# Two 64-row halves for small contractions, whole output rows, and later score steps in an attention-plus-mixer kernel

## The chip, the cores and the metric

The kernel runs on one core of a Trainium2 chip. The metric is the device time of one execution in microseconds (us), as the median of several runs. A core has TensorE (PE, matrix products, with its weight loads shown apart as PEld), VectorE (DVE), ScalarE (ACT), GpSimd (POOL) and SyncE (SP, which here issues most DMAs). Each engine works through its own instructions in order and waits on semaphores for the others.

## What is computed

```python
# q, k, v: (8, 8, 576, 64) float32
scores = q @ k.transpose(0, 1, 3, 2) / sqrt(64)
rel = pos[:, None] - pos[None, :]
mask_plain = (rel >= 0) & (rel < 32)                       # heads 0 to 3
mask_dil = (rel >= 0) & (rel < 128) & (rel % 4 == 0)       # heads 4 to 7
attn = softmax(where(mask, scores, -1e9))
x = (attn @ v).transpose(0, 2, 1, 3).reshape(8, 576, 512)
h = relu(x.transpose(0, 2, 1) @ w_tok1) @ w_tok2           # w_tok1 (576, 256), w_tok2 (256, 576)
u = x + h.transpose(0, 2, 1)
out = u + relu(u @ w_ch1) @ w_ch2                          # w_ch1 (512, 1536), w_ch2 (1536, 512)
```

## The kernel before

Everything is in one Python function that writes out each engine's program by hand; there is no automatic scheduler. Products are in float16 and accumulate in float32 in eight PSUM banks of 512 columns: three named `main`, three `fl` and two `sc`, each group used in turn.

**Stages of one batch.** `transposes` turns casted q and k of a pair of heads into `qz` and `kt` (contraction over 64 features of one head: the two heads of a pair sit in rows 0 to 63 and 64 to 127). Scoring makes the products of keys and queries within the few 128 x 160 blocks that a window touches (heads 0 to 3), within the four residues of 4 (heads 4 to 7, 128 x 128 blocks), and for the 64 tail rows 512 to 575. `values` (names `av`, `rec`, `xn`) multiplies by v with a column of ones, divides, and leaves x in `xn`: four blocks of 128 tokens and a fifth with the 64 tail tokens, in rows 0 to 63 of even batches and 64 to 127 of odd ones. `emit_h1` makes h (`h1p`, then a relu into `h`) in two halves of 256 columns, each for two sets `jb` of the 256 hidden tokens. `emit_u` (`up`) makes u. `gen_main` makes the gate `gt` (`gp` for 128 of the 1536 channels at a time), and the output product: `yp` in batch 0, `yx` and `yw` in `gen_out` for the others. `gen_out` uses differences of the weight blocks, `wsum_a` and `wsum_b`, which `weight_sum` computes once, on VectorE, at the end of batch 0's gating, and adds u and stores `o`.

**Scoring, twice.** From batch 2 on `scores_twin` takes q and k in other tiles (`qt`, `kr`, made by transposing DMAs) and multiplies in 64 rows of the array, the two heads of a pair in the upper and the lower half. Batches 0 and 1 use `scores_plain`, `scores_dil`, `tail_scores` and `score`: `qz` has one copy per head with the other head's 64 rows zero, so each product contracts over 128 rows; and ahead of each product a matmul of the identity with `veil` puts the mask into the bank.

**Order.** The loop over batches takes `gen_main(b)` as the main thread, and `interleave` puts between its pieces a list of steps, each with a due time on a clock of estimated costs and a cost of its own. So in the stretch of `gen_main(0)` the steps of batch 1 run (transposes, scores, values, h1, u), in that of `gen_main(1)` those of batch 2, and so on. Before the loop, batch 0's steps are written out one by one. `w4a` (named `w` in the trace, the second channel weight) comes in three DMAs of 512 KB that GpSimd issues during batch 1's casts. For batches from 2 on, u is turned by transposing DMAs on the sync queue (`utm<-u`), two column blocks of it are copied by ScalarE to `utd`, and `u_natural` turns them back (`u<-utd`) for the addition in `gen_out`.

Of the kernel before, what the change touches and what calls it, by code (L numbers as in the profile page):

```python
# [9 lines left out]
FP16 = mybir.dt.float16  # L10
# [58 lines left out]
def kernel(  # L69
# [64 lines left out]
    qza = fixed("qz", [128, 4, 2, S])  # L134
# [16 lines left out]
    w1t = [fixed(f"w1t{i}", [128, DTOK]) for i in range(2)]  # L151
# [11 lines left out]
    def emit_fixed():  # L163
        nc.gpsimd.memset(idle, 0.0)
        nc.gpsimd.memset(spread, 0.0)
        nc.vector.memset(qza[64:128, :, 0], 0.0)
# [34 lines left out]
    def load_v_steps(b):  # L201
        tn = sb.tile([128, 4, 4, D], FP32, tag="l_vn", bufs=1, name=f"l_vn_{b}")
        td = sb.tile([128, 4, 4, D], FP32, tag="l_vd", bufs=1, name=f"l_vd_{b}")
        tx = sb.tile([128, 4, D], FP32, tag="l_vx", bufs=1, name=f"l_vx_{b}")
# [12 lines left out]
        steps.append(go(tx, v[b, 4:8, 384:512, :].rearrange("h s d -> s h d")))  # L217
# [55 lines left out]
    def cast_vx(b, eng):  # L273
        copy(eng, vt[b % 2][:, :, 0:64], l32[(b, "vx")])
# [30 lines left out]
    def transposes(b, nm, hp):  # L305
# [13 lines left out]
        if b == 0:  # L319
            for h in range(2):  # L320
                rows = slice(64 * h, 64 * h + 64)
                if hp >= 2:
                    copy(eng, qz[hp][rows, h, 0:512], p[rows, 0:512])
                else:
                    copy(eng, natural(qz[hp][rows, h, 0:512]), main[rows])
# [6 lines left out]
        for h in range(2):
            rows = slice(64 * h, 64 * h + 64)
            if flat:
                copy(eng, qz[hp][rows, h], p[rows, 0:S])
            else:
                copy(eng, natural(qz[hp][rows, h]), grid[rows, :, 0:MR].rearrange("p r m -> p m r"))
# [71 lines left out]
    def first_tails():  # L409
# [7 lines left out]
        for h in range(2):  # L417
            rows = slice(64 * h, 64 * h + 64)
            nc.vector.tensor_copy(out=qza[rows, :, h, 512:S], in_=t[rows, :, 0])
        nc.vector.tensor_copy(out=kta[:, :, 512:S], in_=t[:, :, 1])  # L420

    def score(b, hp, h, out, keys, queries, hide):

        if hide is not None:
            nc.tensor.matmul(out=out, lhsT=ident, rhs=hide, start=True, stop=False)
        lhsT = keys if not isinstance(keys, slice) else kt[hp][:, keys]
        nc.tensor.matmul(out=out, lhsT=lhsT, rhs=qz[hp][:, h, queries],
                         start=hide is None, stop=True)

    def veiled(b, hp):  # L430
        return b <= 1

    def small_bank(b, hp):
        return bank("main", 3, f"sm_{b}_{hp}") if b == 0 else bank("sc", 2, f"sm_{b}_{hp}")
# [16 lines left out]
    def tail_scores(b, hp, p, c0):  # L451
        n = len(near(hp))
        for h in range(2):
            for i, x in enumerate(near(hp)):
                c = c0 + 64 * (n * h + i)
                v0 = BLK + 128 * (hp // 2) + 64 * x
                score(b, hp, h, p[:, c:c + 64], near_keys(x), slice(512, S),
                      veil[:, v0:v0 + 64] if veiled(b, hp) else None)

    def tail_exp(hp, p):  # L460
        nc.scalar.activation(
            out=tail_cols(attt[:, hp], hp),
            in_=p[:, 0:128 * len(near(hp))].rearrange("p (h x c) -> p h x c", h=2, c=64), func=AF.Exp, scale=0.125)

    def scores_plain(b, hp):
        blocks = plain_blocks(hp)
        veils = veiled(b, hp)
        for h in range(2):
            p = bank("sc", 2, f"sc_{b}_{hp}_{h}")
            for kb in range(3):  # L470
                score(b, hp, h, p[:, BLK * kb:BLK * kb + BLK], slice(128 * kb, 128 * kb + 128),
                      slice(128 * kb, 128 * kb + BLK), veil[:, 0:BLK] if veils else None)
            nc.scalar.activation(
                out=blocks[:, h, 0:3, 0:BLK], in_=p[:, 0:3 * BLK].rearrange("p (b c) -> p b c", c=BLK),
                func=AF.Exp, scale=0.125)
            yield 0.21
        p = small_bank(b, hp)
        for h in range(2):
            score(b, hp, h, p[:, 128 * h:128 * h + 128], slice(384, 512), slice(384, 512),
                  veil[:, 0:128] if veils else None)  # L480
        tail_scores(b, hp, p, 256)
        nc.scalar.activation(
            out=blocks[:, :, 3, 0:128], in_=p[:, 0:256].rearrange("p (h c) -> p h c", c=128),
            func=AF.Exp, scale=0.125)
        tail_exp(hp, p[:, 256:512])
        if not veils:
            mult(nc.gpsimd, blocks[:, :, :, 0:BLK], blocks[:, :, :, 0:BLK], band)
# [763 lines left out]
```

## Time and profile before

| | |
|---|---|
| median of 3 runs | 280.49 us (279.01 to 281.66) |
| profiled execution | 278.42 us, of which its span is 276.6 us |
| granted TensorE clock in it | 1.00 |
| TensorE busy | 265.8 us, 96% of the span, 2694 matmuls |
| VectorE, ScalarE, GpSimd busy | 168.3, 149.0, 158.8 us |
| DMA | 55.50 MB, mean 201 GB/s |

The profile is one execution. Busy times count overlapping instructions of an engine once; a matmul's shown duration includes its latency, so consecutive ones overlap, and the distance of their starts is what one costs. In the chain of work that ended last each piece is a stretch during which nothing else was waited for; a piece of n matmuls lasts n such distances.

### The profile page before, as it was taken

What the parts mean: (1) busy time and instruction counts of PE and PEld (TensorE: products, weight loads), DVE (VectorE), ACT (ScalarE), POOL (GpSimd) and SP (SyncE); (2) the same over time, 40 slices, a digit from 0 to 9 for tenths busy, and PEclk for the clock granted to TensorE, in tenths of its full rate; (3) what the DMA queues carried; (4) which work ended last, traced back from release to release, by engine and by line L of the source; (5) the groups of instructions that cost most, each with busy time, mean ns of one, the idle gap of its engine ahead of it and who ended that gap; (6) DMA issues with size and microseconds to landing.
All of it is one profiled execution on the core that took longest, in us unless ns stands there. A gap on an engine that the chain in (4) does not pass through costs nothing.

```text
span 276.6 us, 6790 instructions
## 1 busy us (share of the span) xinstructions
PE 265.8 (96%) x2694; PEld 197.2 (71%) x2694; DVE 168.3 (61%) x340; ACT 149.0 (54%) x291; POOL 158.8 (57%) x214
## 2 busy tenths in 40 slices
PE   6899999999999999997999999999999999999994
PEld 2796676897666876685775876687776866786673
DVE  6767668575568655674649454775475473961363
ACT  2864774363674465467545656476546565236500
POOL 7880760389858759849973589739980870000000
PEclk9999999999999999999999999999999999999999
DMA  7999999995979799999999999989999220553015
GB/s 216 271 248 238 291 241 210 316 241 159 343 132 226 151 316 281 233 165 259 304 221 186 257 280 255 172 156 316 304 211 148 81 79 2 99 147 78 0 40 152
DMA packets 116783, 55.50 MB, mean 201 GB/s; under 512 B 84976, under 2 KB 115696, under 8 KB 116752
## 3 DMA queue, kind: packets, MB, share of 16 engines
q1 hardware_dynamic: 112096, 49.63, 75.9%
q0 software_dynamic: 2640, 3.94, 7.9%
q10 hardware_dynamic: 2016, 1.51, 1.8%
q8 instruction: 21, 0.34, 0.5%
q14 instruction: 10, 0.08, 0.1%
HBM read 38.12 MB, written 9.44 MB: 172 GB/s over the span
## 4 chain that ended last, share of the span: by engine, by line
PE 85%; DMA 7%; DVE 4%; issue 1%; ACT 1%; ACTq 0%; POOL 0%; DVEq 0%
PE gp L934 29%; PE yx L778 12%; PE yw L778 9%; PE h1p L637 5%; PE up L649 4%; PE gt L925 4%; PE yp L961 4%; PE yp L747 3%; DMA lt<-in_k_dram 3%; PE sc L522 3%; DMA u<-utd 2%; DMA w1p<-in_moe_w_tok_dram 2%; PE h1p L635 1%; PE av L614 1%; PE av L619 1%; DVE gt L737 1%
## 5 line engine op out<-in xcount | busy, mean ns | idle before, releaser
L109 ACT ACTIVATE gt<-gp 128x512 f16<-128x512 f32 x89 | 53.2, 598 | 50.4 <-PE gp L934 50.1
L778 PEld LDWEIGHTS <-gt 128*128 128x128 f16 x600 | 57.0, 98 | 10.2 <-issue 2.0
L934 PE MATMUL gp<-utd,w 128*128 128x512 f16 x144 | 54.7, 380 | 0.0
L934 PE MATMUL gp<-utm,w 128*128 128x512 f16 x144 | 54.6, 379 | 0.0
L934 PEld LDWEIGHTS <-w 128*128 128x128 f16 x384 | 39.1, 113 | 19.8 <-issue 0.5
L115 POOL TENSOR_TENSOR attp<-attp,const 128x1280 f16<-128x1280 f16 x12 | 31.6, 2637 | 23.4 <-ACT attp L547 23.4
L737 DVE TENSOR_TENSOR gt<-gt 128x768 f16<-128x768 f16 x56 | 32.2, 605 | 12.5 <-ACT gt L109 12.2
L115 DVE TENSOR_TENSOR xn<-av,rec 128x320 f16<-128x320 f32 x64 | 31.4, 491 | 2.2
L115 POOL TENSOR_TENSOR attd<-attd,const 128x1024 f16<-128x1024 f16 x12 | 25.5, 2124 | 7.7 <-issue 5.4
L934 PE MATMUL gp<-uT,w 128*128 128x512 f16 x96 | 25.8, 380 | 0.0
L793 DVE TENSOR_TENSOR o<-yx,u 128x512 f32<-128x512 f32 x22 | 15.2, 689 | 11.2 <-PE yx L778 10.5
L778 PE MATMUL yx<-w,gt 128*128 128x256 f16 x168 | 20.6, 273 | 0.0
L778 PE MATMUL yx<-wsum_a,gt 128*128 128x256 f16 x168 | 20.6, 273 | 0.0
L547 ACT ACTIVATE attp<-sc 128x480 f16<-128x480 f32 (+1 forms) x36 | 15.9, 538 | 8.7 <-PE sc L522 8.7
L655 DVE TENSOR_TENSOR u<-up,xn 128x512 f16<-128x512 f32 x26 | 17.8, 688 | 4.1 <-PE up L649 4.1
L626 DVE RECIPROCAL rec<-av 128x5 f32<-128x5 f32 x64 | 12.2, 191 | 12.2 <-PE av L623 12.1
L105 POOL CAST c_k<-l_k 128x512 f16<-128x512 f32 x29 | 17.6, 616 | 2.2 <-DMA l_k<-in_k_dram 1.3
L863 ACT COPY utd<-utm 128x512 f16<-128x512 f16 x12 | 12.7, 1129 | 10.3 <-DMA u<-utd 6.6
L105 POOL CAST c_q<-l_q 128x512 f16<-128x512 f32 x26 | 16.3, 630 | 2.9 <-DMA l_q<-in_q_dram 2.2
L664 DVE TENSOR_TENSOR u16t<-up,xn 64x512 f16<-64x512 f32 x7 | 4.8, 689 | 21.0 <-PE up L660 21.0
L109 ACT ACTIVATE h<-h1p 128x256 f16<-128x256 f32 x31 | 11.8, 384 | 8.9 <-PE h1p L637 8.4
L798 DVE TENSOR_TENSOR o<-yw,o 128x512 f32<-128x512 f32 x13 | 9.0, 691 | 11.4 <-PE yw L778 11.3
(158 smaller groups left out, 549.6 us busy)
## 6 DMA issues: line engine op xcount, KB each, us to landing
l_q<-in_q_dram SPq DMA_DIRECT2D x15, 512.0 KB, 6.6
l_k<-in_k_dram SPq DMA_DIRECT2D x14, 512.0 KB, 7.4
out_dram<-o SPq DMA_DIRECT2D x26, 256.0 KB, 4.1
l_vn<-in_v_dram SPq DMA_DIRECT2D x32, 128.0 KB, 6.7
l_vd<-in_v_dram SPq DMA_DIRECT2D x16, 256.0 KB, 4.2
w<-in_moe_w_ch_dram POOLq DMA_DIRECT2D x6, 512.0 KB, 7.6
out_dram<-o SPq DMA_DIRECT2D x17, 128.0 KB, 2.7
l_vt<-in_v_dram SPq DMA_DIRECT2D x8, 256.0 KB, 4.7
```

Source lines behind the costliest of these rows:

```text
L105: eng.tensor_copy(out=out, in_=in_)
L109: nc.scalar.activation(out=out, in_=in_, func=AF.Relu)
L115: eng.tensor_tensor(out=out, in0=x, in1=y, op=ALU.mult)
L547: nc.scalar.activation(out=out, in_=in_, func=AF.Exp, scale=0.125)
L626: nc.vector.reciprocal(out=rec[:, :, 0], in_=av[:, :, 64])
L637: nc.tensor.matmul(out=p, lhsT=w[:, s, j], rhs=x[:, s, c], start=False, stop=(s == 3))
L655: nc.vector.tensor_tensor(out=u16(b, s), in0=blocks4(p), in1=blocks4(xn[b][:, s]), op=ALU.add)
L737: nc.vector.tensor_tensor(out=out, in0=x, in1=y, op=op)
L778: nc.tensor.matmul(out=p, lhsT=gta[:, k0 + mb, r:r + 128], rhs=weights[:, mb, c], start=(first and not mb and (not a or len(parts) > 2)), ...
L793: nc.vector.tensor_tensor(out=grid(o[(i, j)]), in0=grid(p), in1=u, op=ALU.add)
L863: nc.scalar.copy(out=natural(uTd[:, cb - 2]), in_=uTm[i][:, cb].rearrange("p r m -> p m r"))
L934: nc.tensor.matmul(out=p, lhsT=w3_block(cb, mb), rhs=uT[(b, cb)][0], start=(i == 0), stop=(i == 3))
```

## The change

1. `qz` has no zero half any more: both heads of a pair lie in one tile of 128 rows, two zeroings go, and q is copied in one instruction instead of two.
2. `scores_veiled` takes the place of the four scoring functions for batches 0 and 1. One mask matmul covers a whole bank (or each of two parts of it); the products are made in 64 rows, the two heads of a pair one behind the other into two banks, and the small blocks of two pairs share two banks. 58 matmuls per batch where there were 88. The due times of these steps are new, and the start's order is written out anew.
3. `emit_h1` makes the main four products of both `jb` first and then the 64 tail tokens for both, in 64 rows each, `jb` 0 from the upper and `jb` 1 from the lower half; both relus follow. `values` copies the tail rows to the other half, once for heads 0 to 3 and once for 4 to 7. `w1t` holds its 64 rows twice, by two DMAs, and needs no zeroing.
4. The tail of v (`l_vx`, `vt`) is loaded and cast for 64 rows only.
5. The output of a batch lies in two tiles of whole rows, single instead of four in turn. Batches 1 to 6 store each in one DMA of 512 KB where there were four of 256 KB.
6. In batch 1 one of the turned blocks of u uses another group of banks.
7. `u_natural(2)` is issued in the stretch of `gen_main(1)` instead of `gen_main(2)`.

```diff
-    qza = fixed("qz", [128, 4, 2, S])
+    qza = fixed("qz", [128, 2, 4, S])[:, 0]
...
-    w1t = [fixed(f"w1t{i}", [128, DTOK]) for i in range(2)]
+    w1t = fixed("w1t", [128, DTOK])
...
-        nc.vector.memset(qza[64:128, :, 0], 0.0)
-        nc.vector.memset(qza[0:64, :, 1], 0.0)
...
-        tx = sb.tile([128, 4, D], FP32, tag="l_vx", bufs=1, name=f"l_vx_{b}")
+        tx = sb.tile([64, 4, D], FP32, tag="l_vx", bufs=1, name=f"l_vx_{b}")
...
+    def scores_veiled(b, g):
+
+        def hide(p, c0, n, v0, w, start=True):
+            nc.tensor.matmul(out=p[:, c0:c0 + n * w].rearrange("p (x c) -> p x c", c=w), lhsT=ident,
+                             rhs=veil[:, v0:v0 + w].unsqueeze(1).broadcast_to([128, n, w]),
+                             start=start, stop=False, skip_group_check=True)
+
+        def pair(hp, banks, c0, keys, queries):
+            for h in range(2):
+                rows = slice(64 * h, 64 * h + 64)
+                q16 = qz[hp][rows, queries]
+                nc.tensor.matmul(out=banks[h][:, c0:c0 + q16.shape[-1]], lhsT=kt[hp][rows, keys], rhs=q16,
+                                 start=False, stop=True, skip_group_check=True)
+
+        n, w = (4, 128) if g else (3, BLK)
+        pairs = (2 * g, 2 * g + 1)
+        for hp in pairs:
+            ps = [bank("sc", 2, f"sc_{b}_{hp}_{h}") for h in range(2)]
+            for p in ps:
+                hide(p, 0, n, 0, w)
+            for i in range(n):
+                pair(hp, ps, w * i, slice(i, 512, 4) if g else slice(128 * i, 128 * i + 128),
+                     slice(128 * i, 128 * i + w))
...
+            yield
...
+        for p in small:
+            hide(p, 0, 2, v0, 64 * m)
+            if not g:
+                hide(p, 256, 2, 0, 128, False)
+        for j, hp in enumerate(pairs):
+            for i, x in enumerate(near(hp)):
+                pair(hp, small, 64 * (m * j + i), near_keys(x), slice(512, S))
+            if not g:
+                pair(hp, small, 256 + 128 * j, slice(384, 512), slice(384, 512))
...
         mult(nc.vector, xn[b][:, :, D * h:D * h + D], av[:, :, 0:64], rec)
-
-    def emit_h1(b, jb, half, t):
+        if h % 4 == 3:
+            c = slice(256 * (h // 4), 256 * (h // 4) + 256)
+            tail = slice(64, 128) if odd else slice(0, 64)
+            other = slice(0, 64) if odd else slice(64, 128)
+            nc.vector.tensor_copy(out=xn[b][other, 4, c], in_=xn[b][tail, 4, c])
+
+    def emit_h1(b, half, t):
...
-        p = bank("fl", 3, f"h1p_{b}_{jb}_{half}")[:, 0:256]
-        nc.tensor.matmul(out=p, lhsT=w1t[b % 2][:, j], rhs=x[:, 4, c], start=True, stop=False)
-        for s in range(4):
-            nc.tensor.matmul(out=p, lhsT=w[:, s, j], rhs=x[:, s, c], start=False, stop=(s == 3))
-        relu(nc.vector if jb and half and b == 0 else nc.scalar, t[:, c], p)
+        p = []
+        for jb in range(2):
+            p.append(bank("fl", 3, f"h1p_{b}_{jb}_{half}")[:, 0:256])
+            for s in range(4):
+                nc.tensor.matmul(out=p[jb], lhsT=w[:, s, jb:DTOK:2], rhs=x[:, s, c], start=(s == 0), stop=False)
+            if not jb:
+                yield
+        for jb in range(2):
+            rows = slice(64 * jb, 64 * jb + 64)
+            nc.tensor.matmul(out=p[jb], lhsT=w1t[rows, jb:DTOK:2], rhs=x[rows, 4, c], start=False, stop=True)
+        for jb in range(2):
+            relu(nc.vector if jb and half and b == 0 else nc.scalar, t[jb][:, c], p[jb])
+        yield
...
+        o = [fixed_o32(f"rows{i}", f"o_{b}_{i}") for i in range(2)]
...
-            store(1, 1)
             yield from product(m0 + 256, 6, wsum[4], False, w)
             with_t(1, 0, [(pw, None, None)])
-            store(1, 0)
+            store(1, every)
             yield from product(o0, 6, w4a[:, 6:12, 256:512], False, x)
             with_u(px, 0, 1)
-            store(0, 1)
+            store(0, every)
...
-            steps += score_steps(1, 0, 0, (0.0, 0.7, 1.5),
-                                 ((3.0, 4.9), (4.3, 6.6), (6.9, 9.2), (8.3, 11.0)))
+            steps += score_steps(1, 0, 0, places=(3.0, 4.3, 6.9, 8.3, 5.1, 6.8, 8.3, 9.7, 11.4, 13.0))
             va = value_steps(1, 13.2, 0.7)
...
-            steps += at(13.5, 0.0, [lambda: u_natural(1)])
+            steps += at(13.5, 0.0, [lambda: u_natural(1)]) + at(27.0, 0.0, [lambda: u_natural(2)])
...
-            steps += at(14.6 + late / 6, 0.0, [lambda b=b: u_natural(b)])
+            if b > 2:
+                steps += at(14.6 + late / 6, 0.0, [lambda b=b: u_natural(b)])
```

The program order is moved in three places. The first is VectorE in the stretch of `gen_main(0)`, where batch 1's values end (`rec` and `xn` of heads 4 to 7 from bank `av`) and the weight sums begin. Before:

```order
L626 RECIPROCAL rec_5_941<-av_5_934 128x5
L115 TENSOR_TENSOR xn_857<-av_5_934,rec_5_941 128x5x64
L626 RECIPROCAL rec_6_954<-av_6_947 128x5
L115 TENSOR_TENSOR xn_857<-av_6_947,rec_6_954 128x5x64
L626 RECIPROCAL rec_7_967<-av_7_960 128x5
L115 TENSOR_TENSOR xn_857<-av_7_960,rec_7_967 128x5x64
L725 TENSOR_TENSOR wsum_a<-w_87 128x1536
L725 TENSOR_TENSOR wsum_a<-w_87,wsum_a 128x1536
```

Now, in the same place:

```order
L594 RECIPROCAL rec_5_884<-av_5_877 128x5
L115 TENSOR_TENSOR xn_802<-av_5_877,rec_5_884 128x5x64
L705 TENSOR_TENSOR wsum_a<-w_86 128x1536
L705 TENSOR_TENSOR wsum_a<-w_86,wsum_a 128x1536
L705 TENSOR_TENSOR wsum_a<-w_86 128x1536
L594 RECIPROCAL rec_6_908<-av_6_901 128x5
L115 TENSOR_TENSOR xn_802<-av_6_901,rec_6_908 128x5x64
L594 RECIPROCAL rec_7_924<-av_7_917 128x5
```

The three sums moved from behind head 7 to between heads 5 and 6.

The second is TensorE at the same stage, at batch 1's h1 (`w1n` and `w1p` are the two halves' token weights, `w1t` those of the tail; `gt` is the gate as stationary operand of `yp`). Before, at the beginning of the second half, with the semaphores waited for in brackets:

```order
L961 LDWEIGHTS gt
L961 MATMUL yp_0_995<-w_87,gt 128x256
L635 LDWEIGHTS w1t_80 [waits DVE_49]
L635 MATMUL h1p_0_1_1003<-xn_857,w1t_80 128x256 [waits PE_49]
L637 LDWEIGHTS w1p
L637 MATMUL h1p_0_1_1003<-xn_857,w1p 128x256
```

Now, at `jb` 1 of the first half, whose bank is that of `av_6`:

```order
L610 LDWEIGHTS w1n
L610 MATMUL h1p_0_0_928<-xn_802,w1n 128x256
L610 LDWEIGHTS w1n [waits DVE_49]
L610 MATMUL h1p_1_0_933<-xn_802,w1n 128x256 [waits PE_49]
L610 LDWEIGHTS w1n
```

and at the end of that half:

```order
L610 MATMUL h1p_1_0_933<-xn_802,w1n 128x256
L615 LDWEIGHTS w1t
L615 MATMUL h1p_0_0_928<-xn_802,w1t 128x256
L615 LDWEIGHTS w1t
L615 MATMUL h1p_1_0_933<-xn_802,w1t 128x256
L948 LDWEIGHTS gt
```

The tail's product stood first in each `jb`; now the two stand together behind the eight others. The wait in the brackets of `h1p_1_0` is for `xn` of head 6.

The third is the sync queue, where u of batch 2 is turned back. Before, in the stretch of `gen_main(2)`:

```order
L353 DMA_TRANSPOSE qt<-c_q_1957 128x8x128
L702 DMA_TRANSPOSE utm_90<-u_3_2104 128x16x128
L708 DMA_TRANSPOSE u_2_1643<-utd 128x8x128
L700 DMA_TRANSPOSE utt<-u16t_95 128x4x128
L198 DMA lt_2176<-in_q_dram 64x8x64
L198 DMA lt_2176<-in_k_dram 64x8x64
```

Now, in the stretch of `gen_main(1)`:

```order
L191 DMA l_q_1_1624<-in_q_dram 128x4x256
L191 DMA l_k_1_1626<-in_k_dram 128x4x256
L208 DMA l_vn_1717<-in_v_dram 128x4x64
L688 DMA_TRANSPOSE u_2_1575<-utd 128x8x128
L208 DMA l_vn_1717<-in_v_dram 128x4x64 x3
L208 DMA l_vt_1720<-in_v_dram 128x8x64
L208 DMA l_vd_1718<-in_v_dram 128x2x256 x2
L791 DMA out_dram<-o_1_1677 128x2x512
```

The turn back moved ahead of the turns of batch 3's u, into the loads of batch 4.

More of the change, by code (lines that the diff above doesn't have):

```diff
@@ L171, in emit_fixed @@
         nc.vector.memset(attt, 1.0)
+        for i in range(2):
+            nc.gpsimd.memset(vt[i][64:128], 0.0)
     def emit_fixed_late():
@@ L319, in transposes @@
         if b == 0:
[L320 to L325, printed above, removed]
+            if hp >= 2:
+                copy(eng, qz[hp][:, 0:512], p[:, 0:512])
+            else:
+                copy(eng, natural(qz[hp][:, 0:512]), main)
             return
@@ L329, in transposes @@
             nc.tensor.transpose(out=p[:, 512:640], in_=tail, identity=ident)
+            copy(eng, qz[hp], p[:, 0:S])
         else:
             nc.tensor.transpose(out=grid[:, :, 128:RS], in_=tail, identity=perm)
[L332 to L337, printed above, removed]
+            copy(eng, natural(qz[hp]), grid[:, :, 0:MR].rearrange("p r m -> p m r"))
         if flat:
@@ L416, in first_tails @@
         t = p[:, 0:512].rearrange("p (x n c) -> p x n c", n=2, c=64)
-        for h in range(2):
-            rows = slice(64 * h, 64 * h + 64)
-            nc.vector.tensor_copy(out=qza[rows, :, h, 512:S], in_=t[rows, :, 0])
+        nc.vector.tensor_copy(out=qza[:, :, 512:S], in_=t[:, :, 0])
         nc.vector.tensor_copy(out=kta[:, :, 512:S], in_=t[:, :, 1])
[L422 to L434, printed above, removed]
     def near(hp):
@@ L465, in scores_plain @@
[L465 to L487, printed above, removed]
-            mult(nc.gpsimd, tail_cols(attt[:, hp], hp), tail_cols(attt[:, hp], hp), tails_mask(hp))
-        yield 0.21
@@ L737, in gate_sums, with fixed_o32 @@
             nc.vector.tensor_tensor(out=out, in0=x, in1=y, op=op)
+    def fixed_o32(tag, name):
+        return sb.tile([128, DM] if tag == "o32" else [128, 2, DM], FP32, tag=tag, bufs=1, name=name)
     def gen_out(b):
@@ L818, in gen_out @@
         with_t(0, 0, [(pw, None, None)])
-        store(0, 0)
+        if last:
+            store(0, left)
         if not ahead:
@@ L876, in score_steps @@
         for hp in range(4):
-            at, at_s = places[hp] if places else (t0 + hp * dt, t0 + hp * dt + dt)
             for nm in ("q", "k"):
-                steps.append((at + 0.9 * (nm == "k"), 0.28, lambda nm=nm, hp=hp: transposes(b, nm, hp)))
-            g = (scores_plain if hp < 2 else scores_dil)(b, hp)
-            for i in range(3):
-                steps.append((at_s + offs[i], 0.42 if veiled(b, hp) else 0.21, lambda g=g: next(g)))
+                steps.append((places[hp] + 0.9 * (nm == "k"), 0.28, lambda nm=nm, hp=hp: transposes(b, nm, hp)))
+        for g in range(2):
+            f = scores_veiled(b, g)
+            for i, cost in enumerate((0.62, 0.62, 0.4)):
+                steps.append((places[4 + 3 * g + i], cost, lambda f=f: next(f)))
         return steps
@@ L951, in gen_main @@
             weight_sum(i)
+        rows = [fixed_o32(f"rows{i}", f"o_{b}_{i}") for i in range(2)]
         for s in range(4):
@@ L1053, in tp @@
     def tp(hp):
[L1054 to L1059 removed]
+        ts[2 * hp]()
+        ts[2 * hp + 1]()
     def natural_w1(i):
```

132 lines of the change are left out of this document (55 added, 77 removed).

## Prediction

> **What bounds the kernel now.** The page comes first: the engines' shares and the chain that ended last.
>
> ```profile
> PE 265.8 (96%) x2694; PEld 197.2 (71%) x2694; DVE 168.3 (61%) x340; ACT 149.0 (54%) x291; POOL 158.8 (57%) x214
> PE 85%; DMA 7%; DVE 4%; issue 1%; ACT 1%; ACTq 0%; POOL 0%; DVEq 0%
> ```
>
> TensorE is busy in 96% of the span and carries 85% of the chain. A change is therefore worth what it does to the time between matmul starts, plus what it does to the few places where TensorE waits. The waits of TensorE and the longest pieces of the chain (start, length, what) name these places:
>
> ```profile
> PE sc L427 <- DVE kt L316: 1.4, 4, 0.5
> PE yw L778 <- DVE o L793: 1.5, 1, 1.5
> PE up L1110 <- ACT h L109: 0.2, 1, 0.2
> 1.80 7.20 DMA lt<-in_k_dram
> 9.61 5.39 DMA w1p<-in_moe_w_tok_dram
> 15.04 1.05 PE w_p L1065 x8
> 119.61 5.71 DMA u<-utd
> ```
>
> Up to 15.04 two loads carry the chain, so TensorE work saved before the first `w_p` ends nothing earlier. After that there are the scoring of batch 1 (1.4 us of waits for keys) and one wait of 1.5 us in batch 2, on a transposing DMA of 5.71 us.
>
> Durations in the groups overlap (a 256-wide matmul shows 272 ns), so I price matmuls by the chain's pieces, which run from start to start. The last three rows here are one visit of the scoring of later batches, from 64 rows of the array, between two pieces of 128-row work:
>
> ```profile
> 47.12 0.43 PE gp L934 x2
> 49.29 0.44 PE h1p L637 x4
> 72.14 0.90 PE gt L925 x16
> 218.72 0.66 PE yw L778 x6
> 219.38 0.67 PE sc L522 x24
> 220.04 0.76 PE yw L778 x6
> ```
>
> A 512-wide matmul costs 0.216 us, a 256-wide one 0.109, a 128-wide one 0.056: 0.43 ns per column at every width. The 24 scoring matmuls are 16 of 128 columns and 8 of 64. One after another they would take 16 x 0.056 + 8 x 0.028 = 1.12 us; they took 0.67. As 12 concurrent pairs they would take 0.56. So pairs do run side by side, but entering 64-row work costs the other 0.11 us, and the six `yw` behind it take 0.76 instead of 0.66, which is 0.10 for going back. **A visit to 64-row work costs 0.21 us**, whatever is done in it.
>
> **The change, part by part.**
>
> *Tail of h1.* Per half batch two 256-wide tail matmuls become one pair: minus 0.109. The pair is a visit of its own, plus 0.21. Net +0.10 us for each of 16 halves; it would have to hold two pairs per visit to break even.
>
> The Trainium skill, page "TensorEngine Tiling (Array Packing)", recommends in When to Use Tiling two row tiles for a contraction of 64, but its Key Properties say "Mode switching requires drain"; the trace agrees with the second (0.21 us per visit), and by the first alone each half would save 0.11 us instead of losing 0.10.
>
> *Scoring of batches 0 and 1.* By the code one batch has 5248 columns of key-query products and as many of masks, in 88 matmuls. Now it has 58: the masks in 14 wide ones, the products in 22 pairs that halve their columns. That saves 2624 x 0.43 ns = 1.13 us a batch, 2.3 for both. Against it stand six visits a batch (four for large blocks, two for small ones), 12 x 0.21 = 2.5 us. TensorE's sum is +0.2. The waits for `kt` (1.4 us) can shrink, since fewer waits stand ahead of separate banks: between 0 and minus 1.0, taken as minus 0.5. Both matter only if TensorE is what comes last in batch 1's values, which it is not, as follows.
>
> *A new wait in batch 1.* The steps of batch 1 are timed later against the channel mixing of batch 0, so VectorE now has the three weight sums between head 5 and head 6 (the order shown above), where they stood behind head 7. VectorE works in order, and the second sum needs a piece of `w` that lands late. VectorE's timeline of before (start, length):
>
> ```profile
> 46.64 0.18 DVE L626 RECIPROCAL rec<-av 128x5 f32<-128x5 f32 x1
> 46.86 0.49 DVE L115 TENSOR_TENSOR xn<-av,rec 128x320 f16<-128x320 f32 x1
> 47.26 0.95 DVE L725 TENSOR_TENSOR wsum_a<-w 128x1536 f16<-128x1536 f16 x1
> 48.72 0.96 DVE L725 TENSOR_TENSOR wsum_a<-w,wsum_a 128x1536 f16<-128x1536 f16 x1 [0.51 <-DMA w<-in_moe_w_ch_dram]
> 49.60 0.95 DVE L725 TENSOR_TENSOR wsum_a<-w 128x1536 f16<-128x1536 f16 x1
> ```
>
> The second sum started at 48.72 on the DMA's arrival. That load's issue and size are untouched and the DMA engines are full there, so I keep 48.72. Two sums at 0.88 from start to start end the block at 50.48; `rec` (0.22 to the next) and `xn` (0.49) of head 6 end at 51.2, at 51.25 with the semaphore. What is queued behind them on VectorE is head 7, its copy and the `o` of L954, and TensorE's h1p_1_0 waits for head 6, since its bank is that of av_6; behind it on TensorE stands everything else, as TensorE is in order too. How late is 51.25? I added up the columns of all matmuls that stand in program order from that point to the end, pairs at the old price: 217.0 us. Before, 217.0 us are left at the start of the second half's h1:
>
> ```profile
> 49.02 0.27 PE L635 MATMUL h1p<-xn,w1t 128*128 128x256 f16 x1
> ```
>
> So the program is 51.25 minus 49.02 = **+2.2 us** late there, and this one figure contains whatever the start, the scoring of both batches and batch 0's two halves did, as long as they make TensorE come earlier than 51.25. Their sum (+0.2, +0.2, minus 0.5, and what is hidden by the loads ahead of 15.04) is far from 2.2. Bounds: if the load lands 2.2 us earlier the term is 0; if it lands 1 us later, +3.2.
>
> *The other 14 halves* (batches 1 to 7): 14 x 0.10 = **+1.4 us**, TensorE having no slack there: the windows below show it full in batch 2's gating.
>
> ```profile
> 101.00:117.00 16.00, 16.00 (x142) 10.51 (x141) 10.07 (x24) 8.50 (x17) 15.10 (x22) 1.00 1.05 270
> ```
>
> From both sides: 14 x (minus 0.11) if a visit were free, 14 x 0.15 if both relus, now behind the pair, hold a bank.
>
> *u of batch 2.* ScalarE's, the sync queue's, VectorE's and TensorE's timelines of before show that wait:
>
> ```profile
> 95.36 2.08 ACT L863 COPY utd<-utm 128x512 f16<-128x512 f16 x2 [3.65 <-DMA utm<-u]
> 119.61 1.69 SPq L708 DMA_TRANSPOSE u<-utd  x1
> 122.73 0.55 DVE L737 TENSOR_TENSOR gt<-gt 128x768 f16<-128x768 f16 x1
> 125.44 0.69 DVE L793 TENSOR_TENSOR o<-yw,u 128x512 f32<-128x512 f32 x1 [2.16 <-DMA u<-utd]
> 123.23 1.47 PE L778 MATMUL yx<-wsum_a,gt 128*128 128x256 f16 x12
> 126.18 0.81 PE L778 MATMUL yw<-wsum_b,gt 128*128 128x256 f16 x6 [1.48 <-DVE o L793]
> ```
>
> The 12 `yx` end their starts at 123.23 + 12 x 0.109 = 124.54; the next `yw` starts at 126.18. The transposing DMA now stands in the sync queue among the loads of batch 4, nearly a batch earlier, and the last copy that writes `utd` is done at 97.4, so it lands well before 119. Late next is VectorE's `o` itself: its source's last matmul starts near 123.1, VectorE is free at 122.73 + 0.55 = 123.28, so it is done by 124.0, ahead of 124.54. The whole gap of **minus 1.64** goes; the least that can go is 0, if the earlier DMA pushes back loads.
>
> *The rest*, at nothing. Two zeroings of `qz` on VectorE (one row of 1.0 us) and the halved copies of `q` lie ahead of 15.04 or beside TensorE. The first two rows here are one of those zeroings and a store; the other two, the nearest to the 16 new copies of 64 x 256:
>
> ```profile
> L166 DVE MEMSET qz<- 64x1152 uint32 x1 | 1.0, 1018 | 1.0 <-PEq L1235 1.0
> out_dram<-o SPq DMA_DIRECT2D x26, 256.0 KB, 4.1
> L105 DVE COPY kt<-tp_q 128x64 f16<-128x64 f16 x3 | 0.6, 201 | 0.0
> L420 DVE COPY kt<-tp_t 128x256 f16<-128x256 f16 x1 | 0.3, 292 | 0.0
> ```
>
> The copies take 0.2 to 0.3 us each; only the pair waits for them, and eight h1 matmuls (0.87 us) stand between; without that cover they would cost 16 x 0.3 = 4.8 us. Stores: two of 512 KB in place of four of 256 KB, late in a batch. TensorE shows no wait for a store; the tiles are single now and written again most of a batch later, against some us of landing (256 KB take 4.1). I take 0, between minus 0.3 (fewer bytes in small packets) and +1.
>
> **Sum**: 2.2 + 1.4 - 1.6 = +2.0 us. Against the profiled execution, 278.4 + 2.0 = 280.4. The median of the runs shown is 280.49, 2.1 above that execution; on its scale the forecast is **282.5 us**. About 1% (2.8 us) is what a measurement of this kernel can tell from no change.
>
> **The rivals.**
>
> *The third piece of w lands earlier, or the sums do not hold head 6.* For it: 64 KB less per batch of v, and two startup zeroings on VectorE fewer. Against it: the load is issued behind others in a full stage. Then the terms are h1 16 x 0.10 = 1.6, scoring 0.2, `kt` waits minus 0.5, u minus 1.6: minus 0.3, so 280.2.
>
> *A visit to 64-row work is free*, as a pair alone would have it. For it: pairs do overlap (0.67 us instead of 1.12). Against it: the 0.76 beside 0.66. Then h1 in 14 halves gives minus 1.5, and with the wait in batch 1, 2.2 - 1.5 - 1.6 = minus 0.9: 279.6; without the wait minus 1.7, minus 2.3, minus 0.5 and minus 1.6 make 274.4. This is the time by the skill's When to Use Tiling alone.
>
> *The other side: relus behind the pair make `up` wait.* Both relus of a half now start after the pair, where the first ran beside the second's matmuls. One relu lasts 384 ns:
>
> ```profile
> L109 ACT ACTIVATE gt<-gp 128x512 f16<-128x512 f32 x89 | 53.2, 598 | 50.4 <-PE gp L934 50.1
> L109 ACT ACTIVATE h<-h1p 128x256 f16<-128x256 f32 x31 | 11.8, 384 | 8.9 <-PE h1p L637 8.4
> ```
>
> Latency 0.27 + 0.30 to the second relu + 0.38 = 0.95 us after the pair's start. In batch 1 there are six 256-wide matmuls (0.66) between the pair and the first `up`, with the pair and the return 0.87. So `up` waits 0.1 us where ScalarE is free and 0.3 to 0.4 where it is in a 598 ns relu of `gt`. With 0.35 in each of seven batches: +2.4 on top, **284.9**. It decides wherever fewer than about seven matmuls lie between pair and `up`.
>
> *The move of u does nothing*, because the sync queue holds it behind a load that waits for its buffer until after 119: 2.2 + 1.4 = +3.6, so 284.1.
>
> **How the numbers follow.** Forecast 0.52; no wait in batch 1 0.22; free visits 0.05; relus 0.17; u unmoved 0.04. The forecast's own bounds are about +0.8 to +3.4, a quarter of it over +2.8. Slower by over 1%: 0.52 x 0.25 + 0.17 + 0.04, less the low end of the last two, 0.32. Faster by over 1%: part of the free visits and the low tail of the second case, 0.06. Within 1%: 0.62. The range 279.3 to 285.1 takes in all but the fastest ends and the upper part of the relus' case.
>
> **What would show it.** In the profile after: `sc` pairs and the h1 tail each with 0.2 us around them; VectorE's `wsum` rows ahead of head 6 and a TensorE wait of 1.5 to 2.3 us at h1p_1_0 between 49 and 51.3; no wait at `yw` near 125; no new wait at `up`. Wrong would be the forecast if the three sums end by 48.5, if visits cost less than 0.1 us, or if TensorE's waits in batches 2 to 7 grow by over 1 us.

## The result, and the profile after

The changed kernel takes 289.55 us in the median of four runs (289.02 to 290.75), the kernel before 279.75 beside it. The ratio is **1.036** (95% interval 1.029 to 1.043): slower by some 10 us, where +2.0 was forecast. The profiled execution took 290.75 us, its span is 288.9; it is 12.3 us longer than the span of before. Two of the four executions took 289.0 us with a granted clock of 0.998, the other two, the profiled one among them, 290.1 and 290.8 us with 0.993; a stretch at a lower clock in the profiled one is shown below.

The page of after, its engines and its chain:

```profile
PE 271.8 (94%) x2634; PEld 189.9 (66%) x2634; DVE 174.6 (60%) x349; ACT 143.4 (50%) x287; POOL 156.6 (54%) x214
PE 72%; DMA 13%; DVE 10%; SPq 2%; issue 1%; POOL 0%; ACTq 0%; ACT 0%; DVEq 0%
```

60 matmuls fewer, and yet TensorE's share of the chain fell from 85% to 72%: the time is in waits for VectorE (4% to 10%) and DMA (7% to 13%). TensorE's waits (total, times, longest) name them:

```profile
PE av L587 <- DVE rec L594: 2.8, 5, 0.6
PE h1p L610 <- DVE xn L115: 2.3, 6, 1.3
PE yp L948 <- DMA w<-in_moe_w_ch_dram: 1.7, 1, 1.7
PE yw L761 <- DVE o L774: 0.9, 1, 0.9
```

The first comes five times and the second six, once in each batch. Of the six only the longest (1.3 us, in batch 1) is the wait that the prediction had; the others are in no term of the sum. To see how much each stage takes, I note in each trace when the gating of a batch starts (first `gp`) and ends (first `yp` or `yx` behind it), and subtract the times of before. This is worked out from the starts of the matmuls, one execution to a column (the profiled one of after is the longest of its four, the one of before is 2.1 us below the median first shown):

```
                   before    after   copies on  mask     old h1   small
                                     ScalarE    in two            parts only
gating 0 starts     26.72    +1.23    +2.92     +1.10    +1.58    +0.02
gating 1 starts     66.99    +5.71    +4.86     +5.28    +3.04    +1.41
gating 2 starts    100.74    +6.10    +4.79     +5.39    +2.68    +1.31
gating 2 ends      117.19    +7.57    +5.16     +5.77    +2.67    +1.31
gating 3 starts    129.57    +5.94    +5.64     +4.37    +1.04    -0.24
gating 3 ends      148.84    +7.25    +5.88     +4.85    +1.03    -0.05
gating 4 ends      178.62    +8.70    +6.25     +5.23    +1.03    -0.05
gating 5 ends      208.62   +10.03    +6.49     +5.73    +1.03    -0.05
gating 6 ends      238.40   +11.48    +6.87     +6.10    +1.03    -0.04
gating 7 starts    247.57   +12.67    +7.70     +7.30    +1.83    -0.04
end                276.63   +12.30    +7.35     +6.96    +1.49    -0.41
```

After loses 1.2 us at the start, 4.5 in batch 0's stretch (with batch 1's values and h1), 0.7 in gating 1, 1.3 to 1.5 in each gating of batches 2 to 6, and 1.2 in the output of batch 6; it gains 1.6 in the output of batch 2. (The columns behind after belong to experiments 1, 3, 7 and 10.)

**The gatings.** VectorE's timeline in gating 3 (values of batch 4), then GpSimd's there:

```profile
139.52 0.49 DVE L115 TENSOR_TENSOR xn<-av,rec 128x320 f16<-128x320 f32 x1
140.04 1.85 DVE L600 COPY xn<-xn 64x256 f16<-64x256 f16 x1
141.93 0.20 DVE L594 RECIPROCAL rec<-av 128x5 f32<-128x5 f32 x1
```

```profile
139.68 2.13 POOL L115 TENSOR_TENSOR attd<-attd,const 128x1024 f16<-128x1024 f16 x1
141.76 0.61 POOL L105 CAST c_t<-lt 128x512 f16<-128x512 f32 x1
```

The copy of tail rows, for which I had taken 0.2 to 0.3 us, lasts 1.85, and ends at 141.90, 83 ns behind the end of GpSimd's multiply at 141.81. The line's own view has its sixteen executions (shortest, median, longest):

```profile
L600 DVE COPY xn<-xn x16: 221/508/1857, 19.0 to 241.7; 64x256 f16<-64x256 f16 x16
```

Alone it takes 221 ns; the six of 1.51 to 1.86 us all began during such a multiply of 2.13 us and ended 0.08 us behind it; four more, of 0.31 to 0.65 us, ended 0.08 to 0.09 us behind a cast of GpSimd. Behind the copy on VectorE stand `rec` and `xn` of heads 4 to 7, and TensorE waits for them, in its timeline:

```profile
142.80 0.28 PE L587 MATMUL av<-vv,attd 128*128 128x65 f16 x4 [0.54 <-DVE rec L594]
143.33 0.61 PE L610 MATMUL h1p<-xn,w1n 128*128 128x256 f16 x4 [0.20 <-DVE xn L115]
143.88 0.28 PE L615 MATMUL h1p<-xn,w1t 64*128 64x256 f16 x2
```

By the starts of the matmuls the gaps are 0.71 and 0.36 us, 1.07 in this gating; and the table, after against the copies on ScalarE, gives 1.07 to 1.10 for each of the five. Of the 0.24 to 0.38 us that are left, 0.20 are the two visits to 64 rows, 0.21 each less 0.11 saved.

The Trainium skill has this rule: "SBUF — State Buffer", section Who interferes with whom, says that VectorE's copies in a mode with two ports and GpSimd exclude each other for whole instructions, and that whoever starts first blocks the other; the trace agrees (end of the copy 0.08 us behind GpSimd's end, six times of six).

The trace of before had such holds already, on other instructions. Nine of its 56 gate differences (VectorE, both inputs in SBUF, median 0.55 us) last 0.73 to 1.46 us, and each of the nine ends 0.40 to 0.42 us behind a copy or cast of GpSimd. The longest, and GpSimd's copy that ended 0.42 us ahead of it, from the two timelines of before:

```profile
146.66 1.46 DVE L737 TENSOR_TENSOR gt<-gt 128x768 f16<-128x768 f16 x1
146.47 1.23 POOL L105 COPY kt<-kr 128x512 f16<-128x512 f16 x1 [2.82 <-PE gp L934]
```

**Batch 0's stretch.** TensorE's timeline shows the forecast wait for head 6, and another ahead of it:

```profile
50.21 0.60 PE L948 MATMUL yp<-w,gt 128*128 128x256 f16 x4 [1.69 <-DMA w<-in_moe_w_ch_dram]
52.78 0.61 PE L610 MATMUL h1p<-xn,w1n 128*128 128x256 f16 x2 [1.35 <-DVE xn L115]
```

and VectorE's shows the arrival of the same load, and head 6 behind the sums:

```profile
50.27 0.96 DVE L705 TENSOR_TENSOR wsum_a<-w,wsum_a 128x1536 f16<-128x1536 f16 x1 [1.04 <-DMA w<-in_moe_w_ch_dram]
52.23 0.49 DVE L115 TENSOR_TENSOR xn<-av,rec 128x320 f16<-128x320 f32 x1
```

The late piece of `w` lands near 50.2, and no longer just ahead of 48.72: GpSimd issued its load 0.9 us later than before, behind casts that wait for loads themselves, and it takes longer. TensorE, which comes to `yp` 1 us earlier than before, waits for it itself, and then for head 6 until 52.78. And in stretches (length, TensorE, weight loads, VectorE, ScalarE, GpSimd; then the granted clock, the DMA share and GB/s):

```profile
48.00:53.00 5.00, 1.97 (x26) 1.37 (x24) 3.89 (x8) 0.00 (x0) 0.78 (x1) 0.98 1.12 267
53.00:56.20 3.20, 3.20 (x17) 1.85 (x16) 0.71 (x2) 0.66 (x2) 2.26 (x4) 0.50 1.10 343
56.20:60.00 3.80, 3.80 (x33) 2.95 (x32) 1.39 (x2) 0.66 (x2) 2.90 (x7) 1.00 1.18 209
```

After the two waits, with 2 of 5 us busy, the clock is 0.50 for 3.2 us: some 1.6 us lost, by an estimate of half of it.

The Trainium skill says in "TensorE: Matmul & The Clock Gate", Part 1, that an idle window of about 3.4 us halves TensorE's clock; here no single wait was that long: by the matmuls' starts the two are 1.85 and 1.5 us, with 1.1 us of matmuls between them.

**u of batch 6.** The wait that left batch 2 came back in batch 6:

```profile
256.88 0.69 DVE L774 TENSOR_TENSOR o<-yw,u 128x512 f32<-128x512 f32 x1 [1.62 <-DMA u<-utd]
```

### The profile page after: what moved, and what is told of

It is laid out like the page before. It is cut to its first block, busy times and chain, and to the rows that moved or that the text cites. A ratio compares the mean times of both kernels' runs of the same rounds, so it can differ in the third digit from the quotient of the medians.

```text
span 288.9 us, 6638 instructions
## 1 busy us (share of the span) xinstructions
PE 271.8 (94%) x2634; PEld 189.9 (66%) x2634; DVE 174.6 (60%) x349; ACT 143.4 (50%) x287; POOL 156.6 (54%) x214
## 3 DMA queue, kind: packets, MB, share of 16 engines
q10 hardware_dynamic: 2016, 1.51, 1.8%
## 4 chain that ended last, share of the span: by engine, by line
PE 72%; DMA 13%; DVE 10%; SPq 2%; issue 1%; POOL 0%; ACTq 0%; ACT 0%; DVEq 0%
PE gp L920 22%; PE yx L761 12%; PE yw L761 8%; PE h1p L610 4%; PE up L629 4%; PE yp L948 4%; DMA w<-in_moe_w_ch_dram 4%; PE yp L730 4%; DVE xn L600 4%; DVE xn L115 3%; PE gt L911 3%; DMA l_vn<-in_v_dram 3%; PE sc L493 3%; DMA lt<-in_k_dram 2%; DMA l_vt<-in_v_dram 2%; DMA u<-utd 2%
## 5 line engine op out<-in xcount | busy, mean ns | idle before, releaser
L920 PEld LDWEIGHTS <-w 128*128 128x128 f16 x384 | 38.3, 114 | 20.2 <-issue 0.5
L717 DVE TENSOR_TENSOR gt<-gt 128x768 f16<-128x768 f16 x56 | 30.3, 571 | 13.4 <-ACT gt L109 13.0
L429 ACT ACTIVATE attp<-sc 128x480 f16<-128x480 f32 (+1 forms) x44 | 20.0, 544 | 13.3 <-PE sc L493 10.0
L109 ACT ACTIVATE h<-h1p 128x256 f16<-128x256 f32 x31 | 10.4, 381 | 24.9 <-PE h1p L615 24.7
L429 ACT ACTIVATE attd<-sc 128x512 f16<-128x512 f32 x32 | 16.8, 617 | 2.8 <-PE sc L442 2.8
```

The source lines that it names most:

```text
L109: nc.scalar.activation(out=out, in_=in_, func=AF.Relu)
L429: nc.scalar.activation(out=out, in_=in_, func=AF.Exp, scale=0.125)
L717: nc.vector.tensor_tensor(out=out, in0=x, in1=y, op=op)
L920: nc.tensor.matmul(out=p, lhsT=w3_block(cb, mb), rhs=uT[(b, cb)][0], start=(i == 0), stop=(i == 3))
```

## The experiments

Ratios are medians against the kernel before on the same chip, in brackets the 95% interval. The sixth was run after the ninth, the others in the order told.

**1. Copies on ScalarE.**

```diff
-            nc.vector.tensor_copy(out=xn[b][other, 4, c], in_=xn[b][tail, 4, c])
+            nc.scalar.copy(out=xn[b][other, 4, c], in_=xn[b][tail, 4, c])
```

> The changed kernel with the 16 copies of tail rows on ScalarE instead of VectorE. Theory A (a copy between SBUF tiles on VectorE is held until GpSimd's running multiply of SBUF tiles ends, and the values of heads 4 to 7 wait behind it): the gating of batches 1 to 6 falls from +1.3 to +1.5 us over before (+0.7 in batch 1) to about +0.2 each, minus 6.5 us, and the wait for u of batch 6 (1.1 us) goes with it: 289.5 - 7.6 = 282. Theory B (the copy costs only because it stands in VectorE's queue ahead of the next head): the same, since it leaves the queue. Theory C (the 64-row visits cost 1.3 us a batch, whatever the copy does): no change, 289.5.

1.032 (1.027 to 1.037). Against the 1.036 of the change the intervals overlap, so the reading rests on the table: the gatings of batches 2 to 6 now lose 0.24 to 0.38 us, so theory C falls and the visits have their price. The total gains less than forecast, 4.9 us between the two profiles instead of 7.6. The start is 1.7 us later, as ScalarE's copies (0.40 us each) stand in its queue there, though batch 0's stretch makes up for that (1.9 us lost instead of 4.5). The wait for u of batch 6 does not go (0.8 us lost in that output instead of 1.2). And in batch 2's output one of VectorE's gate differences, whose two inputs lie in SBUF, now met a GpSimd multiply (of `attp`, 128.14 to 130.76 us; here are VectorE's timeline, then TensorE's):

```profile
128.42 2.75 DVE L717 TENSOR_TENSOR gt<-gt 128x768 f16<-128x768 f16 x1
131.09 0.68 DVE L774 TENSOR_TENSOR o<-yw,u 128x512 f32<-128x512 f32 x1
```

```profile
131.82 1.47 PE L761 MATMUL yw<-wsum_b,gt 128*128 128x256 f16 x12 [1.43 <-DVE o L774]
```

Its neighbours take 0.54, and it ended 0.41 us behind the multiply. The same exclusion took back the 1.6 us that the earlier u had won, and 0.5 more.

**2. The second rows written from PSUM.**

```diff
-        if h % 4 == 3:
-            c = slice(256 * (h // 4), 256 * (h // 4) + 256)
...
-            nc.vector.tensor_copy(out=xn[b][other, 4, c], in_=xn[b][tail, 4, c])
+        nc.vector.tensor_scalar_mul(out=xn[b][other, 4, D * h:D * h + D], in0=av[tail, 4, 0:64], scalar1=rec[tail, 4])
```

> The changed kernel where each head's tail rows are written a second time by VectorE from the PSUM bank (64 x 64, eight small instructions a batch) instead of one copy between SBUF tiles per four heads. Theory A: an input from PSUM is not held; the small instructions last 0.1 to 0.3 us each at any time, and the gatings lose at least 1 us each: 289.5 - 6 = 283 to 285. Theory B: VectorE's queue gets longer by 8 x 0.2 instead of 2 x 0.22 us a batch, so the time stays or rises: 289.5 to 292.

1.067 (1.065 to 1.069): theory B's direction, and more. The views of that line and of TensorE's waits:

```profile
L598 DVE TENSOR_SCALAR xn<-av,rec x64: 276/283/290, 16.9 to 247.7; 64x64 f16<-64x64 f32 x64
```

```profile
PE h1p L608 <- DVE xn L598: 7.5, 7, 4.0
```

With an input from PSUM no instruction was held, 276 to 290 ns for all 64, 28 of them beside GpSimd multiplies: that part of theory A stands. But eight of them lengthen VectorE's chain of values by 2.3 us a batch, and TensorE waits for it. Worked out as in the table, the gatings of batches 2 to 6 lose 0.9 to 1.6 us, about as much as with the held copies; the start loses 4.6 instead of 1.2, and batch 0's stretch 7.1 instead of 4.5. Both matter: the queue, and the hold that made one entry of it long.

**3. GpSimd's multiply in two.**

```diff
-                mult(nc.gpsimd, w, w, band[:, :, :, 0:128])
+                for i in range(2):
+                    mult(nc.gpsimd, w[:, i:i + 1], w[:, i:i + 1], band[:, :, :, 0:128])
```

> The changed kernel with GpSimd's multiply of the dilated heads' scores (2.13 us for two heads) made in two instructions of one head each. Theory A: a held copy ends within 0.1 us of the end of the first of the GpSimd instructions that it overlaps, so the copies of 1.85 and 1.52 us become at most 1.1 us; the gatings of batches 1 to 6 lose 0.4 to 1.5 us each: 289.5 - 3 to 289.5 - 6. Theory B: copies and time are unchanged, 289.5.

1.031 (1.025 to 1.036); again this overlaps with the interval of the change, and the two profiles differ by 5.3 us, within the 3 to 6 forecast. A copy in VectorE's timeline, all of them in their line's view, and GpSimd's timeline:

```profile
138.47 1.02 DVE L601 COPY xn<-xn 64x256 f16<-64x256 f16 x1
```

```profile
L601 DVE COPY xn<-xn x16: 221/323/1035, 18.9 to 236.3; 64x256 f16<-64x256 f16 x16
```

```profile
138.26 2.27 POOL L115 TENSOR_TENSOR attd<-attd,const 128x512 f16<-128x512 f16 x2
```

The copy from 138.47 ended at 139.50, 0.08 us behind the first of the two multiplies (139.42) and 1.0 us ahead of the end of both. Nothing was changed on VectorE, and the gatings of batches 2 to 6 fell from 1.3 to 1.5 us over before to 0.4 to 0.5. That the masked scores are ready earlier is not what gains: in after GpSimd's multiply had ended (141.81) 1 us before TensorE went on (142.80), and VectorE had worked without a pause in between. That shows the hold as the cause, and its price.

**4. The sums behind heads 6 and 7.**

```diff
-        for i in (1, 2, 3):
-            weight_sum(i)
...
+            if s == 1:
+                for i in (1, 2, 3):
+                    weight_sum(i)
```

> The changed kernel with the first three weight sums behind the first block of batch 0's output (behind heads 6 and 7 in VectorE's queue). The wait of h1p_1_0 for head 6 (1.5 us) must go by every theory; the wait of yp for the weight's DMA (1.85 us) stays. Theory D (the half clock from 53.0 to 56.2, which costs some 1.6 us, needs both waits with the little work between): 289.5 - 1.5 - 1.6 = 286.4. Rival E (the DMA's wait alone lowers the clock): 289.5 - 1.5 = 288.0.

1.039 (1.032 to 1.045), no gain. The wait of h1p_1_0 for the sums went as forecast, but its one profile, of the longest of the four executions (292.8 us), has `yp` waiting twice for pieces of `w`, 3.2 us in all: there the wait behind the sums had only covered a wait for the same load, which both theories missed. Whether the shorter executions wait alike is not shown.

**5 and 6. The load of w earlier**, together with experiments 1 and 4, and alone:

```diff
-    for i in (2, 4, 5, 7, 6, 8, 9, 10, 11):
+    for i in (2, 4, 5, 7, 6, 8):
         casts1[i]()
     for i in range(3):
         nc.gpsimd.dma_start(
             out=w4a[:, 4 * i:4 * i + 4],
...
+    for i in (9, 10, 11):
+        casts1[i]()
```

> The changed kernel with the copies on ScalarE, the weight sums behind the first output block, and the three loads of the second channel weight (w) issued ahead of GpSimd's casts of batch 1's v, some 3 us earlier. Theory F (batch 0's output phase is late because the pieces of w land late, at 50.2 and 52.7 with the sums moved): the waits of yp for w go, TensorE does not idle, its clock stays whole there, and the start of batch 1's gating falls from +4.9 us over before (copies on ScalarE) to +1.5 to +2.5: ratio to before 1.010 to 1.018, some 281 to 283. Rival G (the phase is late because batch 1's values and scores stand later, whatever w does, or the load only takes the place of v's): the start of that gating stays at +4 or more, ratio 1.025 to 1.03.

> The changed kernel with only the three loads of w issued ahead of GpSimd's casts of batch 1's v; copies on VectorE and the sums between heads 5 and 6 stay. Theory F (the late pieces of w hold yp and, through the sums, head 6): batch 0's output phase loses both waits and the half clock, from +4.5 us over before to +0.5 to +1.5, and the ratio to before falls by 0.011 to 0.014, from 1.036 to 1.022 to 1.025. If the order of the sums alone holds head 6, 1.5 us of wait stay at h1p_1_0 and the ratio is 1.029 or more.

Together 1.023 (1.018 to 1.027): no wait for `w`, the clock whole, and batch 0's stretch loses only 0.7 us. Gating 1 starts 3.5 us over before, between the two forecasts, with the start late by 2.8. Alone **1.050** (1.045 to 1.055), the worst but one, where theory F had 1.022 to 1.025. In that run GpSimd, whose casts of batch 1's v follow, shows why:

```profile
36.69 1.61 POOL L1130 DMA_DIRECT2D w<-in_moe_w_ch_dram  x3
48.58 0.62 POOL L105 CAST vv<-l_vd 128x512 f16<-128x512 f32 x1 [7.02 <-DMA l_vd<-in_v_dram]
```

and in its stretches the last three columns are the clock, the DMA share and GB/s:

```profile
20.00:30.00 10.00, 9.31 (x94) 6.50 (x92) 6.62 (x19) 4.25 (x10) 2.09 (x5) 1.00 1.14 230
30.00:40.00 10.00, 9.36 (x87) 5.32 (x85) 6.30 (x13) 5.35 (x13) 7.14 (x14) 1.00 1.14 246
```

The DMA share is over 1 from 20 to 40: what is issued earlier makes something else late, here v, which heads 4 to 7 need (its first `l_vd` lands at 48.5 us, in after at 40.4). So in the second run the load takes the place of v's, as rival G has it; theory F is right in the first, where the waits go and the stretch gains.

**7. The old h1 in the changed kernel**: padded tail rows, no copies.

```diff
...
-            f = emit_h1(b, half, h1)
             for jb in range(2):
-                steps.append((at + 0.9 * jb, 0.43 + 0.12 * jb, lambda f=f: next(f)))
+                steps.append((at + 0.9 * jb, 0.55, lambda jb=jb, half=half: emit_h1(b, jb, half, h1[jb])))
...
```

> The changed kernel with the old h1: the tail rows padded to 128 rows, no copies, no 64-row visits in h1. If the hold of the copies (about 1.1 us a batch) and the visits (0.2 us a batch) are what the gatings lost, the gatings of batches 2 to 6 are within 0.15 us of before and the wait for u of batch 6 is gone; what is left is the start and batch 0's output phase (+5 to +6) less 1.6 for u of batch 2: ratio 1.012 to 1.018. If something else of the change (scores, stores, v) slows the gatings, they stay at +0.5 us or more each and the ratio above 1.022.

**1.005** (1.001 to 1.008), better than forecast. By the table gatings 1 to 6 cost nothing over before. So of the 3.6% some 3.1 come with the new h1, its copies, and the wait in batch 0's stretch that its order allows.

**8. The new h1 alone in the kernel before**: the reverse of that edit, with the copies of experiment 1.

```diff
...
+            nc.scalar.copy(out=xn[b][other, 4, c], in_=xn[b][tail, 4, c])
...
+            f = emit_h1(b, half, h1)
             for jb in range(2):
-                steps.append((at + 0.9 * jb, 0.55, lambda jb=jb, half=half: emit_h1(b, jb, half, h1[jb])))
+                steps.append((at + 0.9 * jb, 0.43 + 0.12 * jb, lambda f=f: next(f)))
...
```

> The kernel before with nothing changed but the h1 in two row halves, its copies on ScalarE. By the price of a visit read from the trace of before (0.21 us against 0.109 saved) seven batches lose 0.2 us each and batch 0 some 0.2 to 0.6: +1.6 to +2.0; with the wait for u of batch 6 (0 to 1.2) ratio 1.006 to 1.012. If a visit were free, 16 x 0.109 = 1.7 us would be saved: ratio 0.994. If the relus behind the pair held up as well: +4, ratio 1.014 or more.

1.014 (1.008 to 1.020), above the 1.006 to 1.012 of its forecast and at the figure given for relus that hold `up`. Its gatings lose 0.22 to 0.37 us each, near the visits' price of 0.20 and with no wait for a relu; the start (+1.8) and batch 0's stretch (+1.8) lose the more: `up` of batch 0 waits 1.2 us for relus of h, which are now behind the pair and behind copies on ScalarE. The output of batch 2 gains 1.6 us here too, though u was not moved: its turn back was issued 3.2 us later than in before and landed after 4.9 us instead of 5.7.

**9. The earlier u alone in the kernel before.**

```diff
-            steps += at(13.5, 0.0, [lambda: u_natural(1)])
+            steps += at(13.5, 0.0, [lambda: u_natural(1)]) + at(27.0, 0.0, [lambda: u_natural(2)])
...
-            steps += at(14.6 + late / 6, 0.0, [lambda b=b: u_natural(b)])
+            if b > 2:
+                steps += at(14.6 + late / 6, 0.0, [lambda b=b: u_natural(b)])
```

> The kernel before with nothing changed but the turn back of batch 2's u, issued in the stretch of batch 1. The wait of yw in batch 2 goes, minus 1.6 us: ratio 0.994. If the earlier DMA pushes loads or other turns back and the time is lost later: ratio 1.000.

0.998 (0.995 to 1.001), minus 1.9 us in the profile. The forecast of 0.994 lies just outside the interval (0.9946 to 1.0007), and no change lies inside it.

**10. The small parts alone in the kernel before**: whole-row stores, v's tail in 64 rows, the bank, the earlier u.

```diff
...
+        o = [fixed_o32(f"rows{i}", f"o_{b}_{i}") for i in range(2)]
...
-        steps.append(go(tx, v[b, 4:8, 384:512, :].rearrange("h s d -> s h d")))
+        steps.append(go(tx, v[b, 4:8, 384:448, :].rearrange("h s d -> s h d")))
...
+            steps += at(13.5, 0.0, [lambda: u_natural(1)]) + at(27.0, 0.0, [lambda: u_natural(2)])
...
```

> The kernel before with only the small parts of the change: stores of whole rows from two single tiles, the tail of v in 64 rows, the bank of a turned block, the earlier turn back of batch 2's u. No old theory gives these a cost: minus 1.6 to minus 1.9 us for u of batch 2, 0 to +0.8 if the turn back of batch 6's u lands late as in the other kernels with these stores: ratio 0.994 to 0.998. If the single tiles or the large stores hold VectorE: 1.003 or more.

**0.995** (0.992 to 0.998): the version that beats both kernels, before by 0.5%; its interval overlaps with that of experiment 9 (0.998). In its profile the output of batch 2 gains 1.6 us, and batch 0's stretch loses 1.4, where `tp_q` waits 1.4 us for a cast of q; which part of the edit that comes from is open. The stores cost nothing that can be seen.

**11. Experiment 7 with the earlier load of w**: the edits of 5 and 7 together.

> The changed kernel with the old h1 (padded, no copies, no 64-row visits) and the loads of w issued earlier. The wait of yp for w (1.2 us) goes: ratio 1.0048 less 0.003 to 0.005, so 1.000 to 1.002. Its difference to the kernel with only the small parts is then what the new scoring of batches 0 and 1 is worth: by the price of visits about +0.2 us of TensorE's time, by the start of the gating +1.5.

1.014 (1.008 to 1.020), slower by 1% than without where 0.3 to 0.5% less was forecast, for the reason of 6: `av` waits 3.7 us for v, whose second `l_vd` lands at 49.2 us, in experiment 7 at 41.7.

**12. TensorE kept busy in the two waits.**

```diff
...
+    def fill(n):
+        p = bank("sc", 2, "fill_p")
+        for _ in range(n):
+            nc.tensor.matmul(out=p, lhsT=idle[:, 0:128], rhs=idle, start=True, stop=True)
...
+                    if s == 0 and not half and mb == 8:
+                        fill(7)
...
+                if b == 1 and not half:
+                    fill(6)
```

> The changed kernel with 13 matmuls on a zero tile that nothing reads: seven of 512 columns right ahead of yp's wait for the late piece of w, six right ahead of h1p_1_0. They take the place of idling (1.5 of 1.85 us and 1.3 of 1.5 us). Theory D (TensorE's idling there lowers its clock for some 3 us behind it): the clock stays whole from 53 to 56, the output phase of batch 0 loses about 1.6 us, from +4.5 over before to +2.9, and the ratio falls from 1.036 to 1.030, in every run as the clock's dip goes. Rival H (the clock falls there for another reason, such as load of the chip or the DMAs): the dip and the ratio stay, or the ratio rises by the little the matmuls delay: 1.036 to 1.039.

The stretches of this run:

```profile
50.50:53.00 2.50, 2.50 (x19) 1.40 (x16) 2.30 (x6) 0.03 (x1) 0.61 (x1) 1.00 1.08 350
53.00:56.20 3.20, 3.20 (x29) 2.67 (x29) 0.69 (x1) 1.29 (x4) 1.82 (x4) 1.00 1.16 328
```

The dip is gone, and batch 0's stretch loses 2.4 us instead of 4.5 in this profile, part of it since `w` came 0.9 us earlier. The other traces agree. In the five profiles with a stretch at 0.50 there or close behind (after and experiments 3, 4, 6 and 11) TensorE is busy 2.6 to 3.2 us of the six from 47 to 53; in the four that wait less and have none (1, 5, 7 and 12) it is 4.4 us or more. So the idling goes with the lower clock, and the filling kept it whole. But the ratio is 1.043 (1.039 to 1.047), above both forecasts and no better than after's, so the dip is not what the median hangs on: the six executions lie between 288.8 and 292.7 us, and the profiled one is the shortest.

## Why the prediction was wrong

- **The step that failed first is "The rest, at nothing"**, in the sentence on the 16 copies: "They" took 0.22 to 1.86 us, not 0.2 to 0.3, and not only the pair waits for them, but all of VectorE's values behind them. I priced them by copies that read PSUM (such reads were not held in experiment 2) and I never laid GpSimd's rows beside VectorE's at that place. Price: 1.07 to 1.10 us in each of the gatings of batches 2 to 6 and 0.45 in that of batch 1, 5.9 of the 10.3 us by which the profile is longer than forecast; experiment 3 removes most of it without touching the copies. The prediction's own sign of being wrong, waits in batches 2 to 7 grown by over 1 us, is what the profile shows.
- **The visit's price holds nearly**: 0.20 a batch by the sum, 0.22 to 0.38 measured without the hold (experiments 1 and 8). A visit that is free would have given gains there; none showed.
- **The wait in batch 1**: place and mechanism were right (h1p_1_0 waits for head 6 behind the sums), its size was not, +2.2 against +5.7 with the start. Head 6 was ready at 52.7 instead of 51.25, since the piece of `w` was assumed at its old time in a stage whose DMA queues are full. That is 1.5 of the 3.5 us, and the clock's dip adds some 1.6 in the execution profiled.
- **u of batch 2** goes as worked out, minus 1.6 in the profile of after and minus 1.9 in experiment 9. Experiment 8 lost that wait too without moving u, so it hangs on more than the place of the issue. That another would appear in batch 6 (1.2 us) was in no case.
- **The rivals**: relus behind the pair hold up `up` only in batch 0 (0.5 us), not in seven batches. The wait of batch 1 was there, so the second case falls, and u did move.
- The copies had been bounded from both sides, but by two rows that both read PSUM; the 4.8 us worked out for copies without cover were not taken into the range.

The new scoring, with its due times and the new order of the start, is not where 10 us went, but it does not pay either: experiment 7 has it and is at 1.005, with batch 0's gating 1.6 us later and TensorE waiting 1.2 us for `w`; experiment 10 does not and is at 0.995. Left open is which of its parts makes the start late, and what else batch 0's stretch hangs on: the last experiment lost the dip and not the time.

## What to carry to other kernels

Before a copy between SBUF tiles is put on VectorE, look what GpSimd does at that moment: here the price was the rest of GpSimd's instruction, and as VectorE's queue feeds TensorE, it was paid there. Splitting GpSimd's long instruction took most of it away; reading from PSUM was not held, but eight instructions in place of two cost more. A small contraction in row tiles pays only if a visit to that mode holds enough work: here about 0.2 us has to be saved before the first gain. Where the DMA queues are full, a load issued earlier made another one late here, and cost 1 to 1.4% in two kernels; with the copies and the sums moved too, the time fell.

## What had not been expected of the hardware

The turn back `u<-utd` of 5.7 us in before, whose wait the change was to remove, goes with an instruction load. The DMA view of six microseconds from the issue, in batch 6 of before and of after:

```profile
q1 hardware_dynamic: 3390, 1.04, 80.3%
u<-utd SPq DMA_TRANSPOSE x1, 3.8
```

```profile
q8 instruction: 1, 0.02, 1.0%
u<-utd SPq DMA_TRANSPOSE x1, 5.2
```

In six kernels there are 32 of these transposes outside the loads of batch 4 (the four among those loads took 8.1 to 9.8 us). The 16 without an instruction load (0.02 MB) in that window landed in 3.2 to 3.9 us; all seven of 4.7 us or more had one. Some with one took 3.1. The traces of the other eight kernels fit: 22 without a load took at most 3.9 us, and all nine of 4.7 us or more had one. The loads fall beside other transposes in other kernels, so a change of the program may move such a wait, as here from batch 2 to batch 6. This is a coincidence seen, not a cause tested.
